# A fused attention and mixer kernel: weights decoded another way, a new plan for its first part, and a shifted slot table behind it

## The chip, the cores and the metric

The kernel runs on one core of a Trainium2 chip. The metric is the device time of one execution in microseconds (us), smaller being better. Six actors appear below by the profile's names: PE (TensorE, the matrix multiplies) with PEld (its weight loads, which run beside the multiplies), DVE (VectorE), ACT (ScalarE), POOL (GpSimd) and SP (SyncE, which issues DMA transfers here; its queue is SPq in the profile).

## The reference: what is computed

For 8 batches of 8 heads, 576 positions, 64 channels a head and 32 memory slots, attention goes through a small memory; then comes a token mixer and a channel mixer (here moe) with residuals:

```python
a = softmax(phi, axis=positions)                  # phi [8,8,576,32]
k_m = einsum('bhsm,bhsd->bhmd', a, k)             # and v_m from v
attn = softmax(scale * q @ k_m.T, axis=memory) @ v_m
x = attn.transpose(0, 2, 1, 3).reshape(8, 576, 512)
u = x + (relu(x.T @ w_tok1) @ w_tok2).T           # 576 -> 256 -> 576
out = u + relu(u @ w_ch1) @ w_ch2                 # 512 -> 1536 -> 512
```

q, k, v and phi are 32-bit floats; the four weight matrices arrive as 64-bit floats, so that each word takes 8 bytes of memory and has to be turned into a 32-bit float on the chip.

## The kernel before

**Arithmetic.** Each large product of two 32-bit operands is three products of shorter ones: a value is split in a high part (a rounding, made by ACT) and a low part (what is left, made by DVE or POOL), and high by high, high by low and low by high are added up in PSUM. In names, a final h is the high and a final l the low part (`uh`/`ul`, `hh`/`hl`, `c1h`/`c1l`).

**Weights.** A `Piece` brings one stretch of 64-bit words to SBUF (`rawc` for the channel mixer's w_ch1 and w_ch2, `raww` for the token mixer's), as two 32-bit words each, `low` and `high`. Six steps decode it in place: ACT takes the three top bits of the low word (`low_bits`, L638); DVE shifts the high word left by three and ors the three bits in (`join`, L643); ACT makes the sign from the high word by a steep Tanh (`signs`, L649); DVE clears the top bit and flips bit 30, which mends the exponent (`rebase`, L652); DVE clamps and multiplies by the sign (`apply`, L658); then ACT writes the high part (L665) and POOL the low part (L669) to the weight tiles. There are 4 pieces for w_tok1 and w_tok2 and 12 for the channel mixer, each of those one hidden block f of w_ch1 (512 words a partition in four transfers) together with the same block of w_ch2 (512 words in one transfer).

**Attention.** A `Quad` is four heads of one batch, 16 in all. Its steps on PE are kvp (memory keys and values from phi), Tp (a transpose), sp (scores; two PSUM tiles, one per half of the positions), Ap and Rp (token mixer's first product) and four u products (the token mixer's second product with the residual; each u is read out by ACT as `uh` or `rest` and by DVE as `ul`). Between sp and Ap stands the softmax: S turned and its maximum subtracted on DVE, exp on ACT, sum and multiplication on DVE; then the rows go out to DRAM and come back in another layout (`rows`, `raw`: L500, L505, L508), and ACT and DVE split them (`nat`, L118, L119). kvp, Tp, sp, Ap, Rp and u share two PSUM banks named `at` in turn.

**Channel mixer.** It runs over 9 chunks of 512 tokens and 12 hidden blocks: `cp` is the first product (L149, 12 matmuls into one of two `ch` banks), ACT and DVE read it out as `hh` (L122) and `hl` (L125), and `acc` is the second product (L188, 12 matmuls into four accumulating banks). At a chunk's end DVE adds the accumulators to the residual (`add`, L206), turns the layout and stores.

**Order.** All engines run their instructions in the program's order, which the kernel writes out by hand in two ways. The first part (batches 0 and 1, all weights, chunk 0) is a list of steps with costs, dependences and rooms (buffers); `plan(seed)` simulates the engines, gives each step a rank with some random noise from the seed, and emits the steps by their simulated begin. The rest goes by a table of half slots: a slot is one pair of products, `run(h, k)` calls what `at(h, fn, k=...)` put at half slot h, and the loop for a pair is

```python
high, low = chunks[c].ch1(f)          # cp
run(2 * g - 1, 1); high(); low()
run(2 * g, 0)                         # between cp and acc
before[0].ch2(before[1])              # acc of the block before
run(2 * g, 1); run(2 * g + 1, -1, 0)  # behind acc, ahead of the next cp
```

so an even half slot with k=0 lies between a cp and an acc, an odd one between an acc and the next cp. A quad of batches 2 to 7 has a first half slot r, and its steps stand at fixed distances from it. Quad (2,0) is planned half in the first part and has its r by itself.

## Time and profile before

| what | value |
|---|---|
| times of three runs | 820.14, 817.47, 820.19 us |
| median | 820.14 us |
| profiled execution | 819.32 us, of which 817.5 are the span from its first to its last instruction |
| busy in the span | PE 785.3, PEld 652.0, DVE 421.4, ACT 223.2, POOL 137.2 us |
| mean granted TensorE clock | 0.99 |

PE is busy for 96% of the span, so whatever shortens the run is either less work on PE or less time in which PE stands still or runs at a lower clock. A row of the timeline has the start, the duration, the engine, line and operation, the tiles written and read, the count, and in brackets how long the engine had been idle and what released it.

### The profile page before, as it was taken

How to read it: one execution, taken by the hardware profiler on the slowest of the kernel's cores; microseconds unless marked ns; L12 is line 12 of the kernel's file. 1: busy time of each engine (PE TensorE's matmuls, PEld its weight loads, DVE VectorE, ACT ScalarE, POOL GpSimd, SP SyncE). 2: the span in 40 equal slices, each digit the busy share in tenths (PEclk: the TensorE clock that was granted, in tenths of full speed). 3: DMA queues.
4: the chain of work that ended last, by engine and by line, in shares of the span. 5: the costliest groups of instructions: out<-in, count | busy, mean ns of one | idle time of the engine just before them, and what ended most of it. 6: DMA issues, size and time to landing. Idle time of an engine off the chain costs nothing.

```text
span 817.5 us, 12023 instructions
## 1 busy us (share of the span) xinstructions
PE 785.3 (96%) x4733; PEld 652.0 (80%) x4733; DVE 421.4 (52%) x699; ACT 223.2 (27%) x430; POOL 137.2 (17%) x136
## 2 busy tenths in 40 slices
PE   6698898999999999999999999999999999999997
PEld 4487677877887878787888888888878788888886
DVE  5898977385446543754456444744375313212115
ACT  4565645322222222222213221222123211210110
POOL 2135442300130002100121012101310300202000
PEclk9979999999999999999999999999999999999999
DMA  8999463035331522343323432252314100200202
GB/s 209 234 220 228 117 169 89 1 87 112 77 93 33 117 65 45 75 92 87 61 59 67 116 56 76 51 133 43 88 34 77 29 1 2 52 0 1 52 0 53
DMA packets 171128, 65.41 MB, mean 80 GB/s; under 512 B 112320, under 2 KB 168384, under 8 KB 171072
## 3 DMA queue, kind: packets, MB, share of 16 engines
q1 hardware_dynamic: 169984, 64.13, 35.1%
q8 instruction: 37, 0.61, 0.3%
q10 hardware_dynamic: 1088, 0.52, 0.3%
q14 instruction: 19, 0.16, 0.1%
HBM read 51.64 MB, written 12.98 MB: 79 GB/s over the span
## 4 chain that ended last, share of the span: by engine, by line
PE 87%; DVE 5%; SPq 3%; DMA 3%; issue 1%; ACT 1%; DVEq 0%; ACTq 0%
PE acc L188 34%; PE cp L149 34%; PE u L581 8%; PE Ap L541 3%; DMA rawc<-in_moe_w_ch_dram 2%; PE kvp L355 2%; PE sp L433 1%; PE Rp L560 1%; DVE rawc L643 1%; PE end L188 1%; SPq L926 1%; DVE rawc L658 1%; SPq L274 1%; DMA raww<-in_moe_w_tok_dram 1%; PE kvp L958 1%
## 5 line engine op out<-in xcount | busy, mean ns | idle before, releaser
L188 PE MATMUL acc<-hh,c 128*128 128x512 f32 x832 | 276.8, 394 | 0.0
L188 PEld LDWEIGHTS acc<-hh,c 128*128 128x128 f32 x832 | 157.2, 189 | 32.8 <-DVE o L206 0.5
L125 DVE SCALAR_TENSOR_TENSOR hl<-cp,hh 128x512 fp32r<-128x512 f32 x104 | 71.6, 689 | 203.7 <-ACT hh L122 203.6
L149 PE MATMUL cp<-uh,c1h 128*128 128x512 f32 x432 | 171.5, 397 | 0.0
L149 PE MATMUL cp<-ul,c1h 128*128 128x512 f32 x432 | 168.5, 390 | 0.0
L149 PE MATMUL cp<-uh,c1l 128*128 128x512 f32 x432 | 168.4, 390 | 0.0
L188 PE MATMUL acc<-hl,c 128*128 128x512 f32 x416 | 163.3, 393 | 2.2 <-DVE hl L125 2.2
L122 ACT ACTIVATE hh<-cp 128x512 fp32r<-128x512 f32 x104 | 62.2, 598 | 226.1 <-PE cp L149 226.1
L149 PEld LDWEIGHTS cp<-uh,c1h 128*128 128x128 f32 x432 | 81.1, 188 | 23.8 <-issue 8.2
L149 PEld LDWEIGHTS cp<-uh,c1l 128*128 128x128 f32 x432 | 81.1, 188 | 17.4
L149 PEld LDWEIGHTS cp<-ul,c1h 128*128 128x128 f32 x432 | 81.2, 188 | 15.5
L188 PEld LDWEIGHTS acc<-hl,c 128*128 128x128 f32 x416 | 78.6, 189 | 17.2 <-DVE hl L125 2.5
L200 POOL TENSOR_TENSOR o<-uh,ul 128x512 f32<-128x512 f32 x36 | 46.3, 1315 | 119.8 <-issue 70.7
L479 POOL TENSOR_TENSOR al<-aT,ah 128x576 fp32r<-128x576 f32 x16 | 23.3, 1455 | 255.9 <-issue 176.7
L594 ACT COPY rest<-u 128x288 f32<-128x288 f32 (+8 forms) x48 | 15.3, 320 | 93.0 <-PE u L581 92.0
L581 PE MATMUL u<-w2h,Rh 128*128 128x288 f32 x128 | 38.1, 298 | 0.0
L581 PE MATMUL u<-w2l,Rh 128*128 128x288 f32 x128 | 38.0, 297 | 0.0
L581 PE MATMUL u<-w2h,Rl 128*128 128x288 f32 x128 | 37.9, 296 | 0.0
L308 DVE TENSOR_REDUCE pr<-phi 128x128 f32<-128x640 f32 x27 | 35.1, 1302 | 5.2 <-DMA phi<-in_phi_dram 5.2
L602 DVE TENSOR_TENSOR ul<-u,uh 128x288 fp32r<-128x288 f32 (+8 forms) x48 | 16.8, 355 | 38.7 <-ACT uh L596 38.6
L541 PE MATMUL Ap<-w1h,nat 128*128 128x256 f32 x144 | 29.2, 294 | 1.5 <-DVE nat L1028 1.5
L441 DVE STREAM_TRANSPOSE S<-sp 128x288 f32<-128x288 f32 x32 | 15.0, 478 | 29.9 <-PE sp L433 28.9
(146 smaller groups left out, 968.8 us busy)
## 6 DMA issues: line engine op xcount, KB each, us to landing
out_dram<-rows SPq DMA_DIRECT2D x32, 256.0 KB, 4.8
kv<-in_k_dram SPq DMA_DIRECT2D x15, 512.0 KB, 4.2
kv<-in_v_dram SPq DMA_DIRECT2D x15, 512.0 KB, 5.5
q<-in_q_dram SPq DMA_DIRECT2D x192, 36.0 KB, 2.1
rawc<-in_moe_w_ch_dram SPq DMA_DIRECT2D x48, 128.0 KB, 5.6
rawc<-in_moe_w_ch_dram SPq DMA_DIRECT2D x12, 512.0 KB, 6.7
phi<-in_phi_dram SPq DMA_DIRECT2D x16, 256.0 KB, 4.5
rows<-S SPq DMA_DIRECT2D x48, 72.0 KB, 2.1
```

What stands on the lines that cost most here:

```text
L122: nc.scalar.activation(out=h, in_=ps, func=AF.Relu)
L125: nc.vector.scalar_tensor_tensor(out=l, in0=ps, scalar=0.0, in1=f32(h), op0=ALU.max, op1=ALU.subtract)
L149: nc.tensor.matmul(ps, l[:, a, w], r[:, a], start=a == 0 and x == 0, stop=a == NKK - 1 and x == 2,)
L188: nc.tensor.matmul(ps, l_[f // 2][:, f % 2, a * P : (a + 1) * P], r[:, w], start=f == start and x == 0, stop=f == end - 1 and x == 2,)
L200: nc.gpsimd.tensor_tensor(out=s.o[:, a], in0=f32(s.uh[:, a]), in1=f32(s.ul[:, a]), op=ALU.add)
L308: nc.vector.tensor_reduce(out=m.rearrange("p (i m) -> p i m", i=4), in_=s.pt.rearrange("p i j m -> p i m j"), axis=AX.X, op=op,)
L355: nc.tensor.matmul(s.kvp[32 * i : 32 * i + 32, : 2 * D], s.pt[:n, i, j, :], s.kv[i][:n, :, j, :], start=j == 0, stop=j == NC - 1,)
L479: nc.gpsimd.tensor_tensor(out=s.al, in0=s.aT, in1=f32(s.ah), op=ALU.subtract)
L541: nc.tensor.matmul(ps[:, :TT], a, w, start=x == 0, stop=x == len(mm) - 1)
L581: nc.tensor.matmul(ps[:, :HALF], a, r, start=x == 0, stop=x == len(mm) - 1)
L594: nc.scalar.copy(out=rest[0][:, kk, o : o + HALF - n], in_=ps[:, n:HALF])
L602: nc.vector.tensor_tensor(out=ch.ul[:, kk, to], in0=ps[:, :n], in1=f32(ch.uh[:, kk, to]), op=ALU.subtract)
```

## The change

It has five parts.

1. **Decoding.** ACT writes the three low bits as a float, 2.0 plus so many units of its last place, so that its word has bit 30 set and the three bits at the bottom; the join is an exclusive or, which then flips bit 30 by the way. What is left of `rebase` is clearing the top bit, a `magnitude`, which either DVE does (an AND) or ACT (Abs). The plan gives 7 of the 16 pieces to ACT: w_tok1's large piece, one of w_tok2's two pieces and five of the channel mixer.
2. **Pieces.** A piece of the channel mixer now holds two blocks of w_ch1 (1024 words, four transfers of twice the size) or two blocks of w_ch2. There are still 12.
3. **Planner.** It knows which steps of DVE and which of POOL it treats as excluding each other (`port`), some POOL steps may go to DVE, and the costs, the noise and the seed are others. Two low parts went to DVE, those of one w_ch1 piece and of one w_ch2 block; the low parts of the attention weights (`al`) all stay on POOL.
4. **Chunk 0's first product** runs its 12 matmuls sorted by product: the four that read `c1l` are last.
5. **Slot table.** The quads of batches 2 to 7, but for quad (2,0), have kvp, Tp and sp half a slot later, while nat, Ap, Rp and u stay at their half slots; sm2 (sum, division and the way through DRAM) goes from k=1 of an even half slot to k=0 of the odd one behind it, which is called right after it; only what stands there at k=-1 (the four additions `add`, at a chunk's end) comes in between. Quad (2,0) keeps kvp, Tp and sp and has what follows one half slot earlier.

```diff
-    mask = wp.tile([P, 6], F32, name="mask")
-    nc.gpsimd.memset(mask, 0.0)
+    mask = wp.tile([P, 7], F32, name="mask")
+    nc.gpsimd.memset(mask[:, :6], 0.0)
+    nc.gpsimd.memset(mask[:, 6:], 2.0)
...
+    two = mask[:, 6:]
...
         def mm_1(s, ps, f):
-            for a in range(NKK):
-                for x, (l, r) in enumerate(((c1h, s.uh), (c1h, s.ul), (c1l, s.uh))):
-                    nc.tensor.matmul(ps, l[:, a, w], r[:, a], ...)
+            mm = [
+                (a, x, l, r)
+                for a in range(NKK)
+                for x, (l, r) in enumerate(((c1h, s.uh), (c1h, s.ul), (c1l, s.uh)))
+            ]
+            if not s.c:
+                mm.sort(key=lambda m: m[1])
+            for n, (a, x, l, r) in enumerate(mm):
+                nc.tensor.matmul(ps, l[:, a, w], r[:, a], start=n == 0, stop=n == len(mm) - 1)
...
-        def a_low(s):
+        def a_low(s, eng=nc.gpsimd):
...
         def low_bits(s):
             nc.scalar.activation(
-                out=s.low, in_=s.low.bitcast(U32), func=AF.Copy, scale=THREE_BITS
+                out=f32(s.low), in_=s.low.bitcast(U32), func=AF.Identity,
+                scale=THREE_BITS * 2.0**-22, bias=two,
             )
 
         def join(s):
             nc.vector.scalar_tensor_tensor(
                 out=s.low, in0=s.high, scalar=3, in1=s.low,
-                op0=ALU.logical_shift_left, op1=ALU.bitwise_or,
+                op0=ALU.logical_shift_left, op1=ALU.bitwise_xor,
             )
...
-        def rebase(s):
-            nc.vector.tensor_scalar(
-                out=s.low, in0=s.low, scalar1=0x7FFFFFFF, scalar2=0x40000000,
-                op0=ALU.bitwise_and, op1=ALU.bitwise_xor,
-            )
+        def magnitude(s, eng):
+            if eng == "ACT":
+                nc.scalar.activation(out=f32(s.low), in_=f32(s.low), func=AF.Abs)
+            else:
+                nc.vector.tensor_scalar(
+                    out=s.low, in0=s.low, scalar1=0x7FFFFFFF, scalar2=None, op0=ALU.bitwise_and
+                )
...
     class PartC1:
-        words, loads, move = DM, 4, 2.8
+        words, loads, move = 2 * DM, 4, 4.4
 
         def __init__(s, f):
-            s.w, s.name = slice(f * P, (f + 1) * P), f"c_{f}"
+            s.w, s.name = slice(f * P, (f + 2) * P), f"c1_{f}"
...
         vary = random.Random(seed)
+        for z in steps:
+            z.eng, z.us = z.ways[0]
+            if z.ways[1] and vary.random() < SHARES[z.ways[1][0]]:
+                z.eng, z.us = z.ways[1]
+            z.port = z.shared and z.eng != "ACT"
...
-            t = free.get(z.eng, 0.0)
+            t = max(free.get(z.eng, 0.0), port if z.port else 0.0)
...
+            port = z.end if z.port else port
...
-    NOISE, SEED = 0.2, 192
+    NOISE, SEED = 0.3, 423
+    SHARES = {"DVE": 0.1, "ACT": 0.5}
...
-        z = step("DVE", vs, p.join, z, use=[raw])
+        z = step("DVE", vs, p.join, z, use=[raw], port=True)
         y = step("ACT", us, p.signs, z, use=[raw])
-        z = step("DVE", 0.15 + 0.6e-3 * p.words, p.rebase, z, use=[raw])
-        z = step("DVE", vs, p.apply, y, z, use=[raw])
+        z = step(
+            "DVE", 0.15 + 0.54e-3 * p.words, None, z, use=[raw], port=True, other=("ACT", us)
+        )
+        z.fn = lambda z=z: p.magnitude(z.eng)
+        z = step("DVE", vs, p.apply, y, z, use=[raw], port=True)
...
             l = step(
-                "POOL", 0.15 + 2.3e-3 * part.words, lambda x=x: p.part_low(x), h, use=[raw]
-            )
+                "POOL", 0.15 + 2.25e-3 * part.words, None, h, use=[raw], port=True,
+                other=("DVE", 0.08 + 1.15e-3 * part.words),
+            )
+            l.fn = lambda x=x, l=l: p.part_low(x, nc.vector if l.eng == "DVE" else nc.gpsimd)
...
-                homes[f], PartC1(f), PartC2(f), after=w_c[f - 5][1][:1] if f > 4 else (),
+                homes[f], *((PartC2(f - 1), PartC2(f)) if f % 2 else (PartC1(f),)),
+                after=w_c[f - 5][0][:1] if f > 4 else (),
...
-            r = 2 * NF * b - (15 if Q else 27)
+            r = 2 * NF * b - (14 if Q else 26)
             if b == 2 and not Q:
                 r = 2 * NF
...
             at(r, qd.step_kv)
             at(r + 1, qd.step_T)
             at(r + 2, qd.step_s)
-            at(r + 3, qd.sm2, k=1)
-            at(r + 7, qd.nat, k=1)
-            at(r + 9, qd.step_A)
-            at(r + 10, qd.step_R)
+            at(r + 3, qd.sm2)
+            at(r + 6, qd.nat, k=1)
+            at(r + 8, qd.step_A)
+            at(r + 9, qd.step_R)
             for x in range(4):
-                at(r + 11 + x, qd.step_u, x // 2, x % 2)
+                at(r + 10 + x, qd.step_u, x // 2, x % 2)
```

Two places in the table's part follow, and one in the planned part. In the rows, the numbers behind the names are the tile's own.

On PE, behind the last u of a quad (`u_3_1`, half slot 24b-1), before the change:

```order
L581 MATMUL u_3_1_3232<-w2h,Rh_1_3075 128x288
L581 MATMUL u_3_1_3232<-w2l,Rh_1_3075 128x288
L581 MATMUL u_3_1_3232<-w2h,Rl_1_3076 128x288
L433 MATMUL sp_4_0_3245<-qT_0_3188,kb_0_3209 32x288 x4
L433 MATMUL sp_4_0_3246<-qT_0_3188,kb_0_3209 32x288 x4
L149 MATMUL cp_3_3262<-uh_2713,c1h 128x512
L149 MATMUL cp_3_3262<-ul_2714,c1h 128x512
```

and the same quad's scores after it:

```order
L157 MATMUL cp_3_3207<-uh_2680,c1h 128x512
L157 MATMUL cp_3_3207<-ul_2681,c1h 128x512
L157 MATMUL cp_3_3207<-uh_2680,c1l 128x512
L435 MATMUL sp_4_0_3229<-qT_0_3183,kb_0_3201 32x288 x4
L435 MATMUL sp_4_0_3230<-qT_0_3183,kb_0_3201 32x288 x4
L190 MATMUL acc_2_2522<-hh_2_3118,c_1535 128x512
L190 MATMUL acc_2_2522<-hl_2_3119,c_1535 128x512
```

The scores stood right behind a u product and ahead of a cp; now a transpose (not shown) and a whole cp stand between, and an acc follows.

On DVE, from the turn of these scores on, before:

```order
L441 STREAM_TRANSPOSE S_0_3255<-sp_4_0_3245 128x288
L441 STREAM_TRANSPOSE S_0_3255<-sp_4_0_3246 128x288
L448 TENSOR_REDUCE mx_0_3258<-S_0_3255 128x18
L451 TENSOR_TENSOR S_0_3255<-S_0_3255,mx_0_3258 128x576
L125 SCALAR_TENSOR_TENSOR hl_3_3276<-cp_3_3262,hh_3_3275 128x512
L460 TENSOR_REDUCE sm_0_3291<-S_0_3255 128x18
L461 TENSOR_SCALAR sm_0_3291<-sm_0_3291 128x18
L462 RECIPROCAL sm_0_3291<-sm_0_3291 128x18
L465 TENSOR_TENSOR S_0_3255<-S_0_3255,sm_0_3291 128x576
L471 STREAM_TRANSPOSE aT_0_3304<-S_0_3255 128x576
L206 TENSOR_TENSOR o_3120<-acc_2_2555,o_3120 128x512
L206 TENSOR_TENSOR o_3120<-acc_2_2556,o_3120 128x512
```

and after:

```order
L443 STREAM_TRANSPOSE S_0_3239<-sp_4_0_3229 128x288
L443 STREAM_TRANSPOSE S_0_3239<-sp_4_0_3230 128x288
L450 TENSOR_REDUCE mx_0_3242<-S_0_3239 128x18
L453 TENSOR_TENSOR S_0_3239<-S_0_3239,mx_0_3242 128x576
L208 TENSOR_TENSOR o_3087<-acc_2_2522,o_3087 128x512
L208 TENSOR_TENSOR o_3087<-acc_2_2523,o_3087 128x512
L208 TENSOR_TENSOR o_3087<-acc_2_2524,o_3087 128x512
L208 TENSOR_TENSOR o_3087<-acc_2_2525,o_3087 128x512
L462 TENSOR_REDUCE sm_0_3262<-S_0_3239 128x18
L463 TENSOR_SCALAR sm_0_3262<-sm_0_3262 128x18
L464 RECIPROCAL sm_0_3262<-sm_0_3262 128x18
L467 TENSOR_TENSOR S_0_3239<-S_0_3239,sm_0_3262 128x576
```

The four additions to the accumulators (`o`) came behind the softmax's sum and turn, and now come ahead of them. `hl` (L125) of the next block stood in between and now comes behind.

On DVE in the planned part, around the first `hl`, before:

```order
L652 TENSOR_SCALAR rawc_371<-rawc_371 128x1024
L943 TENSOR_REDUCE mc_0_715<-mt_0_689 128x1
L945 TENSOR_SCALAR dg_0_717<-ident,mc_0_715 128x128
L658 SCALAR_TENSOR_TENSOR rawc_371<-rawc_371 128x1024
L643 SCALAR_TENSOR_TENSOR rawc_420<-rawc_420 128x1024
L643 SCALAR_TENSOR_TENSOR rawc_454<-rawc_454 128x1024
L125 SCALAR_TENSOR_TENSOR hl_0_739<-cp_0_701,hh_0_738 128x512
```

and after:

```order
L604 TENSOR_TENSOR ul_591<-u_0_1_669,uh_590 128x224
L659 TENSOR_SCALAR rawc_0_372<-rawc_0_372 128x1024
L664 SCALAR_TENSOR_TENSOR rawc_0_372<-rawc_0_372 128x1024
L961 TENSOR_REDUCE mc_0_723<-mt_0_682 128x1
L963 TENSOR_SCALAR dg_0_725<-ident,mc_0_723 128x128
L127 SCALAR_TENSOR_TENSOR hl_0_721<-cp_0_690,hh_0_720 128x512
```

Two joins and an apply that stood right ahead of the first `hl` are gone from there; one AND and one apply stand further up.

More of the change, by code (lines that the diff above doesn't have):

```diff
@@ L368, in scales @@
             nc.vector.reciprocal(out=sm, in_=sm)
[L369 removed]
+            nc.vector.tensor_scalar_mul(out=s.ms, in0=mask[:, :6], scalar1=sm)
             s.per = sm
@@ L751 @@
     class PartC2:
-        words, loads, move = DM, 1, 2.4
+        words, loads, move = DM, 1, 2.2
         held = []
@@ L792, with __init__ @@
     class Step:
-        def __init__(s, eng, us, fn, after, take, use, move):
+        def __init__(s, eng, us, fn, after, take, use, move, port, other):
             s.eng, s.us, s.fn, s.after, s.take, s.move = eng, us, fn, list(after), take, move
+            s.port = s.shared = port or eng == "POOL"
+            s.ways = [(eng, us), other]
             s.begin = s.end = s.ready = None
@@ L803, with step @@
     steps = []
-    def step(eng, us, fn, *after, take=(), use=(), move=0.0):
-        steps.append(Step(eng, us, fn, after, list(take), list(use), move))
+    def step(eng, us, fn, *after, take=(), use=(), move=0.0, port=False, other=None):
+        steps.append(Step(eng, us, fn, after, list(take), list(use), move, port, other))
         return steps[-1]
```

39 lines of the change are left out of this document (17 added, 22 removed).

## The prediction

> **What bounds the kernel now.** I read the page first, then the busy time by stretches, then what PE waits for in each, then the timeline at these waits.
>
> ```profile
> PE 785.3 (96%) x4733; PEld 652.0 (80%) x4733; DVE 421.4 (52%) x699; ACT 223.2 (27%) x430; POOL 137.2 (17%) x136
> 0.00:59.70 59.70, 42.46 (x381) 36.38 (x382) 45.71 (x74) 32.16 (x60) 14.04 (x30) 0.91 0.97 223
> 59.70:159.70 100.00, 91.96 (x606) 75.45 (x607) 74.47 (x99) 52.96 (x87) 42.38 (x31) 0.98 0.51 126
> 159.70:802.00 642.30, 641.40 (x3676) 531.02 (x3675) 292.42 (x509) 138.06 (x284) 80.75 (x76) 1.00 0.28 60
> 39.80:49.90 10.10, 8.55 (x38) 8.09 (x38) 9.20 (x11) 5.44 (x9) 4.61 (x4) 0.50 1.11 230
> 98.00:101.00 3.00, 3.00 (x9) 2.32 (x9) 2.96 (x6) 2.39 (x5) 1.29 (x2) 0.50 0.00 0
> ```
>
> Ahead of the stretches' engines (PE, PEld, DVE, ACT, POOL) stands the length, behind them the granted clock, the DMA share and GB/s. Three stages with different limits: up to 59.7 us DMA is at 0.97 of its time and PE idles 17 us, so the first product waits for loads and decoding. From there to 159.7 PE idles 100 - 91.96 = 8.0 us and has a stretch at half clock. Behind it PE idles 0.9 us in 642, and only its own rows can hide a loss. PE's matmul count does not change in any of them, so the sum is made of waits.
>
> ```profile
> PE mt L939 <- DVE nat L1028: 2.5, 1, 2.5
> PE acc L188 <- DVE hl L125: 2.2, 1, 2.2
> PE u L581 <- DVE Rl L125: 1.7, 1, 1.7
> PE np L1015 <- DVE phi L322: 0.9, 1, 0.9
> PE mt L939 <- DVE pr L308: 0.5, 1, 0.5
> PE u L581 <- DVE mc L943: 0.5, 1, 0.5
> PE u L581 <- DVE ul L602: 0.3, 1, 0.3
> PEld sp L433 <- DVE ul L602: 3.0, 4, 0.9
> PEld sp L433 <- ACT rest L594: 2.8, 7, 0.4
> ```
>
> The first seven are PE's waits from 59.7 to 159.7, all on DVE, 8.6 in all against 8.0 of idle time, since a wait can begin beside a matmul's end; the last two are weight loads' waits behind 159.7, which the busy share hides because a matmul row runs on while its loads wait.
>
> **The slot table.** Scores as they run unhindered (169.96), and behind a u whose readout by ACT they await (420.98); the row at 189.79 closes six products:
>
> ```profile
> 169.96 0.71 PE L433 MATMUL sp<-qT,kb 64*32 64x288 f32 x16
> 170.60 0.50 PE L188 MATMUL acc<-hh,c 128*128 128x512 f32 x1
> 173.47 0.39 PE L149 MATMUL cp<-uh,c1h 128*128 128x512 f32 x1
> 189.79 0.28 PE L541 MATMUL Ap<-w1h,nat 128*128 128x256 f32 x1
> 420.98 1.25 PE L433 MATMUL sp<-qT,kb 64*32 64x288 f32 x16
> 421.08 0.40 ACT L594 COPY rest<-u 128x288 f32<-128x288 f32 x1 [3.47 <-PE u L581]
> 421.53 0.15 PEld L433 LDWEIGHTS sp<-qT,kb 64*32 64x32 f32 x8 [0.40 <-ACT rest L594]
> 422.15 0.50 PE L149 MATMUL cp<-uh,c1h 128*128 128x512 f32 x1
> ```
>
> The second score tile needs the bank of the u just issued. From their start to the next product's, the scores take 0.64 us at 169.96 and 1.17 at 420.98. By the two rows on sp, 4 + 7 = 11 of the twelve quads from (2,0) on wait, 5.8 us together. The change puts a whole cp between u and scores in ten of them, and its 2.7 us outlast the readout (0.40 us on ACT; DVE's share is of that size, since no wait is over 0.9). In quad (2,1) a u still stands ahead, and up to 0.9 remains. Gain 5.8 - 0.9 = 4.9; I take 5. It may be 6.2, since each loses some 0.13 more than its wait (1.17 - 0.64 - 0.40), ten times. It may be 3.5, if the transpose Tp, now right behind the last u, waits 0.15 in each for its operand from DVE: T is written one product ahead of it now as before, so I take this for the bound only.
>
> What is late next is nat, for which Ap waits; here the moved steps lose room:
>
> ```profile
> 167.71 2.45 DVE L206 TENSOR_TENSOR o<-acc,o 128x512 f32<-128x512 f32 x4
> 174.93 0.75 DVE L460 TENSOR_REDUCE sm<-S 128x18 f32<-128x576 f32 x1
> 177.12 1.99 SPq L500 DMA_DIRECT2D rows<-S  x4
> 184.39 1.05 DVE L119 TENSOR_TENSOR nat<-raw,nat 128x512 fp32r<-128x512 f32 x2
> ```
>
> From the sum's start to nat's end it is 184.39 + 1.05 - 174.93 = 10.5 us, with the rows' way through DRAM in it: four writes issued at 177.12, two reads behind their landing. In the first quads of batches 3 to 7 the four additions (2.45 us on DVE) now precede the sum. They need the acc behind the scores to end, and that took 173.47 - 170.60 = 2.87. So nat is ready 2.87 + 2.45 + 10.5 = 15.8 us behind the scores. Between scores and Ap stand this acc and five products; six products took 189.79 - 173.47 = 16.3, so one is 2.72, and the room is 2.87 + 5 x 2.72 = 16.5. The slack is 0.7 us (before, the sum did not wait for an acc and the room was a product longer). Nothing is moved past another transfer: SP's issues behind the first part stand in the same order, with these writes ahead of the next quad's q. The second quads have no additions and some 2 us of slack. Expected loss 0; where landing takes a microsecond longer, Ap waits for the rest, in five quads.
>
> **The first part.** First the wait of `acc` at the first block:
>
> ```profile
> 65.40 0.48 PE L188 MATMUL acc<-hh,c 128*128 128x512 f32 x1
> 65.05 2.33 DVE L643 SCALAR_TENSOR_TENSOR rawc<-rawc 128x1024 int32<-128x1024 int32 x1
> 67.30 0.68 DVE L125 SCALAR_TENSOR_TENSOR hl<-cp,hh 128x512 fp32r<-128x512 f32 x1
> 68.03 0.50 PE L188 MATMUL acc<-hl,c 128*128 128x512 f32 x1 [2.16 <-DVE hl L125]
> 70.66 0.39 PE L149 MATMUL cp<-uh,c1h 128*128 128x512 f32 x1
> ```
>
> This acc took 70.66 - 65.40 = 5.27 us from start to start, 2.4 to 2.55 more than one that waits for nothing (2.87 or 2.72). `hl` stood behind an apply and two joins; in the changed order the joins are elsewhere, and the maximum `mc` and the small product `dg` come between the apply and it: 2.2 us saved. Of the other six waits the two large ones had their cause in the order of PE: the transpose of phi (mt) behind a pair of np tiles, whose banks it had to get back from nat (2.5), and the u products right behind a cp that follows Rp (1.7). In the changed order an acc stands between the np tiles and the next attention step, and an acc between each Rp and the next u. The four small ones (2.2 together) have a product in between in most cases. What comes instead I followed through the changed order of DVE, ACT and POOL with these durations:
>
> ```profile
> L643 DVE SCALAR_TENSOR_TENSOR rawc<-rawc 128x1024 int32<-128x1024 int32 x12 | 18.0, 1503 | 5.0 <-ACT rawc L638 5.0
> L658 DVE SCALAR_TENSOR_TENSOR rawc<-rawc 128x1024 f32<-128x1024 f32 x12 | 18.1, 1506 | 1.2 <-ACT rawc L649 0.8
> L652 DVE TENSOR_SCALAR rawc<-rawc 128x1024 int32<-128x1024 int32 x12 | 10.4, 863 | 0.2
> L638 ACT ACTIVATE rawc<-rawc 128x1024 int32<-128x1024 uint32 x12 | 13.7, 1146 | 2.6 <-issue 1.4 <-DMA rawc<-in_moe_w_ch_dram 1.3
> L649 ACT ACTIVATE rawc<-rawc 128x1024 int32<-128x1024 f32 x12 | 13.9, 1161 | 3.2 <-DVE rawc L643 3.2
> L669 POOL TENSOR_TENSOR c1l<-rawc,c1h 128x512 fp32r<-128x512 f32 x12 | 17.8, 1484 | 51.9 <-ACT c1h L665 33.5 <-DMA rawc<-in_moe_w_ch_dram 16.5 <-DMA q<-in_q_dram 1.9
> ```
>
> I find 0.2 on a low part of w_ch2, 0.1 on phi's exp, 0.5 on Tp, and allow 2 more for joins that a POOL step stretches (2.33 us at 65.05 against a mean of 1.50). Waits of 8.0 become 2.8, and the half clock goes with the wait of 2.5 us right ahead of it: at 98.00 PE is busy for 3.0 us at 0.50, which costs 1.5. That is 5.2 + 1.5 = 6.7, taken as 6.5; the bounds are 9.5 (no wait, full clock) and 0 (as many new waits as old ones).
>
> The prices of the edits themselves: DVE loses seven `rebase` (five at 0.86, one large and one small at about 0.8), 6 us, and gains two low parts, 2 to 3 us. ACT gains seven Abs like the Tanh beside them, five at 1.16 and two at up to that, some 7.6 us, and saves a start on six joined CASTs. Over 0 to 159.7 ACT is busy 32.16 + 52.96 = 85.1 us; with 93 it still idles 40%, and this idle time is the cover. If it is gone, see the ACT rival. The Identity in place of the Copy is priced as Tanh, 1161 against 1146 ns: nothing. Here the Trainium skill, "ScalarE: Activation LUTs", in the section on what a table load costs, speaks against the change: an operand given by a pointer, as the bias `two` is, adds about 93 ns to an activation; by it ACT would have 1.5 us more in 16 pieces, an estimate from that page, which no run here shows and which the same idle time would cover. Sorting chunk 0's first product moves no work: 0. Fewer, larger transfers move the same bytes under a DMA share of 0.97: 0.
>
> Before the first product, PE waits longest at the first of these rows, right ahead of the half clock, and last at the second:
>
> ```profile
> 38.99 0.44 PE L1015 MATMUL np<-ident,aT 128*128 128x128 f32 x2 [3.22 <-DVE aT L471]
> 59.61 0.33 PE L939 MATMUL mt<-ident,pr 128*128 128x128 f32 x1 [0.49 <-DVE pr L308]
> ```
>
> In the changed order the last u's readout, not this maximum (`pr`), stands last ahead of the first product on DVE, so the 0.49 goes, and the second quad's nat comes earlier on DVE while its aT comes later. I take 1 us off. The bounds are 1 us more (aT later by one step of DVE, nothing won) and 3.3 us less (two thirds of the 10.1 us at half clock from 39.80 on run at full clock, which halves them).
>
> **Sum:** 5 + 6.5 + 1 = 12.5 us off the profiled 819.3 gives 806.8; the median of the runs shown is 0.8 above it. I say 807.
>
> **The rivals.**
>
> - *The first part gives its gain back.* A plan's durations leave out what the trace shows, such as a join of 2.33 us where POOL works. Then only the table's 5 us stay: 814.3. For it: all seven waits were on DVE, and the plan can be off by a microsecond at any of 23 products. Against: DVE has 3 to 4 us less to do in a stretch where it idles a quarter. 0.12.
> - *Ap waits in place of the scores.* With rows home a microsecond or more late in five quads: 806.8 + 5 to 6 = 812.5. For it: a slack of 0.7. Against: no Ap waits behind 159.7 in the trace of before. 0.10.
> - *Full clock throughout.* If the wait of 3.2 us for aT, which ends where the half clock sets in, becomes shorter, PE keeps its clock from 39.80 on. It was busy 8.55 us there at half speed, so up to 4.3 us are won, of which loads (DMA at 1.11) take back a part: some 3 us, 803.7. For it: aT's place on DVE has changed. Against: aT still comes behind the joins of the first weights. 0.12. The Trainium skill, "TensorE: Matmul & The Clock Gate", Part 1 on the clock gate, states a free-running window of 3413 ns, with half speed behind a window without work and full speed behind a busy one; by that rule, this case happens once the wait no longer fills a window. The trace agrees as far as it goes: 10.1 us at half speed are about three such windows, behind a wait of 3.2.
> - *The change does nothing.* Every wait is replaced, and an engine that is busy 96% stays so: 820. Against: the scores' waits depend on the order alone. 0.05.
> - *Slower: ACT's queue becomes the wait.* `hh` stands in ACT's order among Abs, CASTs and Tanh of over a microsecond each; a late `hh` delays `hl` and the acc behind it by as much as at 65.40, 2.55 us. The change is off the gain from five late ones on (12.5 / 2.55), slower than can be told from seven on, and with nine of twelve it is 819.3 - 12.5 + 23 = 830. For it: ACT gets 7.6 us more of work. Against: it idles 47 of the 100 us. 0.04.
>
> My forecast has 0.57. The first, second and fourth case lie at 812 and above and the third a little below it, so the range goes from 802 (4.8 of the 6.6 that the favourable bounds, 1.3 + 3.0 + 2.3, give together) to 815.5, which leaves out the fourth and fifth and the far ends. A measurement of this kernel can tell 0.5%, 4.1 us, from no change: faster is below 816. The first three cases and the forecast make 0.91, less 0.04 for the first one's upper edge: faster 0.87; same 0.08; slower 0.05.
>
> **What would show it.** In the changed profile: scores that take 0.65 us start to start in all quads but (2,1), and no wait of their loads on `rest`; PE idle of 2 to 4 us in the hundred behind the first product; DVE's magnitude in nine pieces; PE never waiting for nat behind 160. It is wrong if PE waits for `hh` in several blocks of chunk 0, if Ap waits for nat, or if the first product begins over 2 us later than at 59.71.

## The result, and the profile after

The changed kernel takes 804.47 us in the median of four runs (804.24 to 804.88), the kernel before 819.96 in the runs beside it: a ratio of 0.9823, with a 95% interval of 0.9808 to 0.9839. The prediction was 807.0, in a range of 802.0 to 815.5. The profiled execution took 804.88 us, of which 803.1 are the span: 14.4 less than the one before. Some executions were disturbed and took at least a fifth longer; all times here are medians of the others, and where the profiled execution was a disturbed one (the slot table alone, and the changed kernel once more) the stages are missing.

First the page's busy times and its stretches, cut where the stages change: ahead of the first product of chunk 0 (57.2 us), from there to the scores of quad (2,0) (161.9), and behind them. The stretch at 39.5 is where the half clock was.

```profile
PE 777.0 (97%) x4737; PEld 646.4 (80%) x4737; DVE 410.2 (51%) x694; ACT 230.7 (29%) x431; POOL 136.1 (17%) x129
0.00:57.20 57.20, 41.51 (x385) 34.22 (x386) 41.61 (x70) 36.68 (x63) 14.99 (x31) 0.97 0.97 236
57.25:161.94 104.69, 100.72 (x723) 82.43 (x723) 75.50 (x112) 57.49 (x90) 35.46 (x23) 1.00 0.51 129
161.90:787.60 625.70, 625.34 (x3558) 520.56 (x3558) 284.29 (x496) 136.47 (x279) 85.60 (x76) 1.00 0.28 60
39.50:50.00 10.50, 7.47 (x58) 7.03 (x57) 9.48 (x11) 8.60 (x14) 4.82 (x4) 1.00 1.04 272
```

The order is PE, PEld, DVE, ACT, POOL, then the granted clock, the DMA share and GB/s. PE's idle time in the middle stage is 104.69 - 100.72 = 4.0 us, and the clock is 1.00 there and at 39.5, where it had been 0.50. ACT has 7.5 us more to do over the run, DVE 11 less. The prediction counted 7.6 and 3 to 4: it took DVE's rows at their old durations, and joins, applies and some other steps are shorter in the mean here.

Next what PE waits for in the middle stage (us in total, times, longest):

```profile
PE sp L1021 <- ACT qT L1011: 1.3, 1, 1.3
PE Ap L543 <- DVE nat L1046: 1.2, 1, 1.2
PE mt L957 <- DVE pr L310: 0.9, 1, 0.9
PE Tp L986 <- DVE vb L392: 0.6, 1, 0.6
PE qt L1003 <- issue: 0.4, 1, 0.4
PE qp L998 <- ACT kb L990: 0.4, 1, 0.4
```

And from the timeline three of the twelve pairs of scores, the last two with the product behind them:

```profile
161.94 0.72 PE L435 MATMUL sp<-qT,kb 64*32 64x288 f32 x16
197.75 0.69 PE L435 MATMUL sp<-qT,kb 64*32 64x288 f32 x8
198.81 0.69 PE L435 MATMUL sp<-qT,kb 64*32 64x288 f32 x8 [0.36 <-DVE ul L604]
199.43 0.50 PE L190 MATMUL acc<-hh,c 128*128 128x512 f32 x1
412.56 0.71 PE L435 MATMUL sp<-qT,kb 64*32 64x288 f32 x16
413.21 0.50 PE L190 MATMUL acc<-hh,c 128*128 128x512 f32 x1
```

None of the seven waits of before is in this list, but for mt on pr. That one stands just ahead of the first product, at 57.16 us, so the stage itself has the other five, some 4 us in all. The scores take 413.21 - 412.56 = 0.65 us to the next product in eleven quads of twelve. Only quad (2,1), at 197.75, still has a u right ahead and takes 1.68.

The span falls into three stages by two events that every profile here has: the first product of chunk 0, and quad (2,0)'s scores, which are the first step of the slot table that is the same in all kernels. Starts are those of the timeline's rows; the last column is the span less the scores' start.

| kernel | first product at | middle stage | scores of (2,0) at | rest |
|---|---|---|---|---|
| before | 59.71 | 110.25 | 169.96 | 647.5 |
| changed | 57.25 | 104.69 | 161.94 | 641.2 |
| difference | -2.5 | -5.6 | -8.0 | -6.4 |

### The profile page after: what moved, and what is told of

It reads as the page before. It is cut to its first block, busy times and chain, and to the rows that moved or that the text cites. A ratio compares the mean times of both kernels' runs of the same rounds, so it can differ in the third digit from the quotient of the medians.

```text
span 803.1 us, 11970 instructions
## 1 busy us (share of the span) xinstructions
PE 777.0 (97%) x4737; PEld 646.4 (80%) x4737; DVE 410.2 (51%) x694; ACT 230.7 (29%) x431; POOL 136.1 (17%) x129
## 4 chain that ended last, share of the span: by engine, by line
PE 88%; DMA 4%; DVE 3%; SPq 3%; issue 1%; ACT 1%; DVEq 0%; ACTq 0%
PE cp L157 35%; PE acc L190 35%; PE u L583 8%; PE Ap L543 3%; DMA rawc<-in_moe_w_ch_dram 2%; PE kvp L357 2%; DMA phi<-in_phi_dram 1%; PE Rp L562 1%; PE end L190 1%; SPq L944 1%; PE sp L435 1%; DVE rawc L647 1%; SPq L276 1%; SPq L280 0%; DVE rawc L664 0%
## 5 line engine op out<-in xcount | busy, mean ns | idle before, releaser
L190 PEld LDWEIGHTS acc<-hh,c 128*128 128x128 f32 x832 | 156.2, 188 | 39.4 <-issue 7.3
L157 PE MATMUL cp<-uh,c1h 128*128 128x512 f32 x432 | 164.7, 395 | 0.0
L157 PE MATMUL cp<-ul,c1h 128*128 128x512 f32 x432 | 162.8, 390 | 0.0
L157 PE MATMUL cp<-uh,c1l 128*128 128x512 f32 x432 | 162.3, 389 | 0.0
L157 PEld LDWEIGHTS cp<-uh,c1h 128*128 128x128 f32 x432 | 80.4, 188 | 16.4 <-issue 0.9
L202 POOL TENSOR_TENSOR o<-uh,ul 128x512 f32<-128x512 f32 x36 | 46.1, 1308 | 117.3 <-DMA out_dram<-rows 46.7
L343 POOL PARTITION_ALL_REDUCE psr<-pr x11 | 17.4, 1585 | 78.1 <-PE cp L157 68.2
```

The lines of the kernel that those rows point to most:

```text
L157: nc.tensor.matmul(ps, l[:, a, w], r[:, a], start=n == 0, stop=n == len(mm) - 1)
L190: nc.tensor.matmul(ps, l_[f // 2][:, f % 2, a * P : (a + 1) * P], r[:, w], start=f == start and x == 0, stop=f == end - 1 and x == 2,)
L202: nc.gpsimd.tensor_tensor(out=s.o[:, a], in0=f32(s.uh[:, a]), in1=f32(s.ul[:, a]), op=ALU.add)
L343: nc.gpsimd.partition_all_reduce(s.r, m, P, RED.add)
```

## The experiments

Twelve runs, in three groups, each group on one chip with runs of the kernel before between them. Ratios are to these, with a 95% interval. All stages are in one table behind the last group.

### Parts apart

**The slot table alone**, on the kernel before:

```diff
-            r = 2 * NF * b - (15 if Q else 27)
+            r = 2 * NF * b - (14 if Q else 26)
...
-            at(r + 3, qd.sm2, k=1)
-            at(r + 7, qd.nat, k=1)
-            at(r + 9, qd.step_A)
+            at(r + 3, qd.sm2)
+            at(r + 6, qd.nat, k=1)
+            at(r + 8, qd.step_A)
```

> The kernel before with the new slot table alone; its first part is unchanged. Theory (the two parts add): from quad (2,0) on to the end the changed kernel was 6.4 us shorter than before (641.2 against 647.5 us), 6.2 of it in the scores, so here the same: 6.0 to 6.5 us less than before, a ratio of 0.992 to 0.993, with scores of 0.65 us start to start everywhere but in quad (2,1). Rival (the table's gain leans on the first part, since the first part's stores and loads of batch 2 run into it): under 4 us, and waits of Ap or kvp behind 160 us.

Measured: 812.32 us against 819.58, a ratio of 0.9913 (0.9883 to 0.9943). **The first part alone**, the changed kernel with these lines turned back:

> The changed kernel with the old slot table; its first part is the changed one. Theory (the parts add): the first product begins 2.5 us earlier (57.2) and quad (2,0)'s scores 8 us earlier than before (162 against 170), then the scores cost as much as before: 7.5 to 8.5 us less than before, a ratio of 0.990 to 0.991. Rival: over 10 us less, if the remaining clock loss of before (half clock around 40 and 98 us) is worth more than the profile's 8 us.

Measured: 811.90 us, 0.9913 (0.9881 to 0.9945). The two gains, 7.3 and 7.7 us, add up to 14.9 before rounding, and the changed kernel has 15.5: the parts add, as far as intervals of 5 us tell. The profiles tell more. The first part alone leaves a rest of 647.6 us, that of before to 0.1; every kernel with the new table and without a further edit has 641.1 to 641.2. So the table is worth 6.4 us, whatever stands ahead of it.

**The planner alone**, on the kernel before: decoding, pieces, first product and slot table are old, but DVE's port steps (the ones that the change marks) and POOL's exclude each other in the plan, and the seed is the best of some 3000 by its planned end. The planner also takes the changed kernel's noise and its costs for the decoding steps, which are 2 to 8% lower; the lines below leave the costs out.

```diff
-            t = free.get(z.eng, 0.0)
+            t = max(free.get(z.eng, 0.0), port if z.port else 0.0)
...
+            port = z.end if z.port else port
...
-        z = step("DVE", vs, p.join, z, use=[raw])
+        z = step("DVE", vs, p.join, z, use=[raw], port=True)
...
-    NOISE, SEED = 0.2, 192
+    NOISE, SEED = 0.3, 1661
```

> The kernel before with its own decoding, pieces and slot table, but planned by a planner that lets DVE's port steps and POOL's steps exclude each other (with the changed kernel's costs for them), under the seed with the best planned end of some 3000. Its plan puts the first product at 58.8 and the last second product of chunk 0 at 152.4 us. The kernel before was planned at 56.0 and 150.9 and ran at 59.7 and 155.7: 3.7 and 4.8 late. The changed kernel was planned at 58.4 and 149.5 and ran at 57.2 and 147.6: 1.2 and 1.9 early. Theory P (the planner's knowledge of the exclusion is the first part's gain): it runs where it is planned or a little earlier, the last second product begins at 150.5 to 152.5, so 3 to 5 us less than before. Rival D (the gain is the lighter decoding on DVE): it stays within 1.5 us of before, 155 or later.

Measured: 812.00 us, 0.9921 (0.9889 to 0.9952): 7.6 us less, more than theory P asked for, and all of what the whole first part brings. **The reverse**, the changed kernel planned without the exclusion:

```diff
-            z.port = z.shared and z.eng != "ACT"
+            z.port = False
...
-    NOISE, SEED = 0.3, 423
+    NOISE, SEED = 0.3, 2507
```

> The changed kernel with all of its decoding, pieces and slot table, but planned without the exclusion of DVE's port steps and POOL's, under the seed with the best planned end of some 2000. Its plan puts the first product at 57.0 and the last second product of chunk 0 at 148.1 us, ahead of the changed kernel's own plan (58.4 and 149.5). Theory P: it runs 4 to 5 us behind its plan as the kernel before did, the last second product begins at 152 to 153, so it is 4 to 6 us slower than the changed kernel, around 809. Rival D (the lighter decoding is the gain): it runs as the changed kernel, 804 to 805.

Measured: 806.52 us, 0.9848 (0.9805 to 0.9890), 2.1 above the changed kernel's median, with intervals that overlap; theory P had asked for 809. The rows of the scores of (2,0), of the first of these kernels and then of the second:

```profile
162.57 0.71 PE L433 MATMUL sp<-qT,kb 64*32 64x288 f32 x16
```

```profile
166.01 0.72 PE L435 MATMUL sp<-qT,kb 64*32 64x288 f32 x16
```

They begin 7.4 and 4.0 us before those of before (169.96). Theory P had the direction of both against their plans, not the sizes: the first begins its last second product at 148.4, 4.0 ahead of its plan (152.4) and ahead of the range expected; the second at 151.7, 3.6 behind (148.1), less than the 4 to 5 expected. Rival D falls as it was put, since the old decoding gets the whole gain.

That the exclusion by itself makes the gain is not shown. With the old decoding no run separates it from the costs and the noise. In the reverse run, which keeps those, the times don't tell a loss, and in the profile what it loses lies ahead of the first product (62.16, where five kernels with the same first part have 55.3 to 59.0); its middle stage of 103.85 us is no longer than the changed kernel's 104.69. Of the 7.4 us of the first kernel, too, 5.3 lie ahead of the first product (54.45 against 59.71) and 2.1 behind it. Nor are its joins shorter than those of before, which took 1503 ns in the mean:

```profile
L643 DVE SCALAR_TENSOR_TENSOR rawc<-rawc 128x1024 int32<-128x1024 int32 x12 | 19.2, 1603 | 4.0 <-ACT rawc L638 2.4 <-DMA rawc<-in_moe_w_ch_dram 1.6
```

### Seed, clock and the one pair of scores left

**The kernel before under another seed** of its own planner:

```diff
-    NOISE, SEED = 0.2, 192
+    NOISE, SEED = 0.2, 387
```

> The kernel before with nothing changed but the seed of its plan: the one of 3000 with the best planned end by its own planner (which knows nothing of the exclusion of DVE and POOL). Its plan puts the first product at 55.9 and the last second product of chunk 0 at 149.0 us, 1.9 ahead of the plan of before (150.9). The run planned without the exclusion but with the new decoding was 4.0 us ahead of before at quad (2,0)'s scores. Theory S (that was the seed: a search over more seeds finds a luckier plan): this one is 2 to 5 us less than before too, its last second product begins at 151 to 153.5 us. Theory D' (that was the lighter decoding): it runs within 1.5 us of before or slower, the last second product at 154 or later, 5 or more behind its plan.

Measured: 820.12 us against 818.68, a ratio of 1.0019 (1.0001 to 1.0037). Planned 1.9 us ahead of before, it begins its last second product at 156.5, 7.5 us behind its plan and 0.8 behind before. The best planned of 3000 seeds is worth nothing to the old planner; theory S falls as it was put, by this one seed.

**Planner and slot table together**, with old decoding, pieces and first product, and under the planner's second-best seed (1113):

> The kernel before with its own decoding and pieces, planned with the exclusion of DVE's port steps and POOL's, under the seed with the second best planned end (first product planned at 58.6, last second product at 152.7), and with the new slot table. Theory P (planner and slot table are the whole gain, decoding and pieces are worth nothing by themselves, and any well placed seed will do): 804 to 806.5 us, as the changed kernel, a ratio of 0.981 to 0.984; the last second product 2 to 4 us ahead of its plan, at 148.5 to 151. Rival (the seed run before was a lucky one, or the decoding is worth something): 808 or more, the last second product behind 152.

Measured: 804.64 us, 0.9838 (0.9807 to 0.9869), against the changed kernel's 804.47 and 0.9823. Its last second product begins at 147.6, 5.1 ahead of its plan, where 2 to 4 had been expected. Two of the five parts, the planner without its choice of engines and the slot table, bring the whole gain as far as the intervals tell, and under a second seed.

**The clock.** In the kernel before, 13 more idle matmuls fill the wait of 3.2 us ahead of the second quad's np:

```diff
                 z.fill = int(0.42 * gap / 0.24)
             idle = z.end
+    c.x_n.fill += 13
     for z in order:
         now[0] = z
```

> The kernel before with 13 more idle matmuls (identity by identity, into a bank that np takes next) ahead of the second quad's np, so that PE works through its wait of 3.2 us for aT at 36 to 39 us. Nothing else moves. Theory: the half clock from 39.7 to 49.9 us comes from the nearly idle stretch before it, so it goes, PE's own work there (8.6 us at half speed) takes some 4 us less, but the first product waits for decoded weights and for DVE as well: 1 to 2.5 us less than before, the first product at 57.2 to 58.7. Rival 1 (the clock is not the limit there at all): first product within 0.5 us of 59.7 at full clock, no gain. Rival 2 (the clock falls for another reason): half clock stays at 39.7.

Measured: 818.24 us against 818.68, 0.9992 (0.9969 to 1.0015): no gain that shows, in an interval from 2.5 us less to 1.2 more. Its stretches, in the columns as above:

```profile
32.70:36.10 3.40, 3.40 (x17) 2.54 (x14) 3.07 (x6) 1.25 (x3) 1.42 (x1) 0.50 1.09 224
36.10:39.50 3.40, 3.40 (x31) 3.40 (x30) 1.93 (x5) 2.62 (x4) 0.00 (x0) 0.94 1.08 235
39.50:43.00 3.50, 3.50 (x33) 3.50 (x32) 3.40 (x5) 2.19 (x5) 1.44 (x2) 1.00 1.09 230
43.00:46.40 3.40, 0.76 (x6) 0.56 (x6) 3.23 (x5) 1.48 (x3) 1.96 (x2) 1.00 1.16 207
46.40:50.00 3.60, 3.60 (x19) 3.60 (x19) 3.57 (x5) 2.21 (x3) 1.29 (x2) 0.55 1.10 218
50.00:53.00 3.00, 3.00 (x25) 3.00 (x24) 2.53 (x4) 2.37 (x5) 0.00 (x0) 0.98 1.11 226
```

And the wait for nat and the first product in its timeline:

```profile
45.86 0.51 PE L541 MATMUL Ap<-w1h,nat 128*128 128x256 f32 x2 [2.64 <-DVE nat L1028]
...
60.44 0.47 PE L149 MATMUL cp<-uh,c1h 128*128 128x512 f32 x1
```

Behind the filled stretch the clock is full at 39.5, so the fall at 39.7 did come from the nearly idle stretch, and rival 2 is out. PE then waits for nat longer, 2.64 us where it had been 1.55. That leaves 43.0 to 46.4 with 0.76 us of work, and the next 3.6 us run at 0.55. The first product begins at 60.44, no earlier than at 59.71.

That is not yet rival 1, because this execution was late before the filler. Its clock is at 0.50 in 32.7 to 36.1, where the kernel before has 1.00. On ACT, `Ah` waits for PE's slowed Ap, the exp of S stands behind it, and DVE waits for the exp:

```profile
36.85 0.37 ACT L1036 CAST Ah<-Ap 128x256 fp32r<-128x256 f32 x1 [2.90 <-PE Ap L541]
37.12 0.69 ACT L456 ACTIVATE S<-S 128x576 f32<-128x576 f32 x1
37.84 0.75 DVE L460 TENSOR_REDUCE sm<-S 128x18 f32<-128x576 f32 x1 [1.37 <-ACT S L456]
40.00 0.78 DVE L471 STREAM_TRANSPOSE aT<-S 128x576 f32<-128x576 f32 x1
45.13 0.99 DVE L1028 TENSOR_TENSOR nat<-np,nat 128x512 fp32r<-128x512 f32 x2
```

The last two of them in the kernel before:

```profile
38.15 0.78 DVE L471 STREAM_TRANSPOSE aT<-S 128x576 f32<-128x576 f32 x1
43.29 0.99 DVE L1028 TENSOR_TENSOR nat<-np,nat 128x512 fp32r<-128x512 f32 x2
```

From aT to nat it is 5.13 us in the filled kernel and 5.14 before, although PE's clock is full in one until 46.7 us and falls to half at 39.7 in the other. On this way DVE is the limit, and a faster PE waits for it. But aT begins 1.85 us later here, and from nat to the first product it is 15.3 us against 16.4. So rival 1 holds for the way to nat; what a full clock is worth for the whole stage, neither this profile nor the times tell.

The Trainium skill, "TensorE: Matmul & The Clock Gate", Part 1 on the clock gate, has half speed behind an idle free-running window of 3413 ns and full speed behind a busy one. The rises, at 50.0 us before and at 36.5 and 50.1 here, stand behind 3.4 us that are full of work. The falls, at 39.7 before and at 29.7 and 46.7 here, stand behind 3.4 us with 0.7, 1.1 and 0.8 us of work, so the trace agrees if an idle window need not be empty.

**Quad (2,0)'s last two u products half a slot later**, in the changed kernel, so that none stands ahead of quad (2,1)'s scores:

```diff
-                at(r + 10 + x, qd.step_u, x // 2, x % 2)
+                at(r + 10 + x + (r == 2 * NF and x > 1), qd.step_u, x // 2, x % 2)
```

> The changed kernel with quad (2,0)'s last two u products one half slot later, so that no u stands ahead of quad (2,1)'s scores, the one place where the scores still take 1.67 us from start to start instead of 0.65. Theory: 1.0 us less than the changed kernel, all scores at 0.65, about 803.4. Rival: the wait goes to the moved u's or to Ap of quad (2,1), no gain.

Measured: 802.93 us, 0.9820 (0.9782 to 0.9858). The pair that took 1.68 us:

```profile
195.68 0.71 PE L435 MATMUL sp<-qT,kb 64*32 64x288 f32 x16
196.32 0.50 PE L190 MATMUL acc<-hh,c 128*128 128x512 f32 x1
```

It takes 0.64 now, and the rest is 640.2 us instead of 641.2. The 1.0 us is shown by the stage; by the times alone it is not, as the group below says.

### On one chip with the changed kernel

**The changed kernel once more:**

> The changed kernel itself, beside the three others on one chip, to compare them with: 804 to 805 us, a ratio of 0.981 to 0.984; its first product begins between 56 and 59 us, as it did at 57.2 here, 59.0 and 55.9 in two kernels with the same first part.

Measured: 803.23 us against 817.53, 0.9821 (0.9790 to 0.9851).

**Its order held, but magnitudes all on DVE and chunk 0's first product unsorted:**

```diff
-        z.fn = lambda z=z: p.magnitude(z.eng)
+        z.fn = lambda: p.magnitude("DVE")
...
-            if not s.c:
-                mm.sort(key=lambda m: m[1])
```

> The changed kernel with its order of steps held, but all magnitudes as an AND on DVE (seven Abs less on ACT, some 7.6 us, seven ANDs more on DVE, some 6 us) and without the sorting of chunk 0's first product. Theory P (the order that the plan finds is the gain; which engine makes the magnitude and the sorting are worth little): within 2 us of the changed kernel, 804 to 806.5, the first product within the 56 to 59 us that equal first parts show. Rival D (DVE is the engine that holds the first part back, and ACT's share of the decoding is what lightens it): 5 to 6 us slower, 809 to 811, with new waits of PE on hl, nat or join.

Measured: 805.63 us, 0.9843 (0.9816 to 0.9871), 2.4 above the changed kernel, a little over the 2 of theory P, in intervals that overlap. Its middle stage, to be held against the changed kernel's row of 57.25 to 161.94 above:

```profile
58.33:163.07 104.74, 100.97 (x723) 82.37 (x723) 77.52 (x116) 54.13 (x88) 35.16 (x23) 1.00 0.51 128
```

ACT has 3.4 us less there, DVE 2.0 more, and the stage is as long to 0.05 us. The first product is at 58.33, inside of what equal first parts show (55.3 to 59.0 in the table). Who makes the magnitude, and whether the product is sorted, moves nothing that can be measured. Rival D's 809 to 811 did not come.

**A later softmax**, some 2.3 us in five quads:

```diff
-            nc.vector.tensor_reduce(out=s.sm, in_=s.S, axis=AX.X, op=ALU.add)
+            for _ in range(4 if s.b > 2 and not s.Q else 1):
+                nc.vector.tensor_reduce(out=s.sm, in_=s.S, axis=AX.X, op=ALU.add)
```

> The changed kernel with the softmax's sum made four times instead of once on DVE in the first quads of batches 3 to 7, which delays their nat by three times 0.75 us, 2.25. Theory (nat is ready only some 0.5 us ahead of Ap in these five quads, 0.80, 0.31, 0.68, 0.07 and 0.65 by the changed kernel's trace, 1.6 to 2.4 in the others): Ap waits 1.7 us for nat in each, 8.7 us in all, so 812 to 814. Rival (there is other room, a DMA landing that hides it or an S that is waited for anyway): under 3 us.

Measured: 811.86 us, 0.9928 (0.9904 to 0.9952), 8.6 above the changed kernel; the rest is 649.2, 8.0 more, 1.6 in each of the five quads. The size is about as expected (8.7), the place is not. From the timeline of one quad, starts in us:

```profile
247.19 3.10 DVE L463 TENSOR_REDUCE sm<-S 128x18 f32<-128x576 f32 x4
251.63 0.78 DVE L474 STREAM_TRANSPOSE aT<-S 128x576 f32<-128x576 f32 x1
252.44 0.67 ACT L478 CAST ah<-aT 128x576 fp32r<-128x576 f32 x1 [6.84 <-DVE aT L474]
253.02 1.08 ACT L124 ACTIVATE hh<-cp 128x512 fp32r<-128x512 f32 x2
253.66 0.51 PE L190 MATMUL acc<-hh,c 128*128 128x512 f32 x1 [0.78 <-ACT hh L124]
```

And what the weight loads wait for behind 161 us, in all five quads:

```profile
PEld acc L190 <- ACT hh L124: 6.0, 5, 1.2
PEld acc L190 <- DVE hl L127: 2.7, 5, 0.5
PEld Ap L544 <- DVE nat L121: 0.2, 1, 0.2
```

`ah`, the split of the softmax's turned tile, stands ahead of `hh` in ACT's order. It waits for aT, `hh` waits behind it, and the acc waits for `hh` and `hl` long before Ap would wait for nat. Once acc has paid 1.6 us, nat is in time to 0.2 us.

**The u products apart, once more:**

> The changed kernel with quad (2,0)'s last two u products one half slot later, once more, beside the changed kernel on the same chip. It had 802.9 us, 1.5 less than the changed kernel's four times. Theory: 1.0 us less than the changed kernel, that is the one pair of scores that took 1.67 us instead of 0.65. Rival: no difference from it, the 1.5 having been the first part's spread.

Measured: 803.00 us, 0.9811 (0.9772 to 0.9851), 0.2 below the changed kernel on this chip, with intervals that overlap. Its rest is 640.2 again. The 1.0 us is shown by the stage in two profiles; the times cannot tell it from the spread.

### All stages

| kernel | first product at | middle stage | scores of (2,0) at | rest | last second product, planned | measured |
|---|---|---|---|---|---|---|
| before | 59.71 | 110.25 | 169.96 | 647.5 | 150.9 | 155.7 |
| before, other seed | 59.12 | 111.65 | 170.78 | 648.0 | 149.0 | 156.5 |
| before, wait filled | 60.44 | 109.99 | 170.44 | 647.5 | 150.9 | 156.2 |
| planner alone | 54.45 | 108.11 | 162.57 | 647.6 | 152.4 | 148.4 |
| planner and slot table | 58.06 | 103.77 | 161.83 | 641.2 | 152.7 | 147.6 |
| changed, planned without exclusion | 62.16 | 103.85 | 166.01 | 641.1 | 148.1 | 151.7 |
| changed | 57.25 | 104.69 | 161.94 | 641.2 | 149.5 | 147.7 |
| first part alone | 59.03 | 104.92 | 163.95 | 647.6 | 149.5 | 149.6 |
| changed, plain decoding | 58.33 | 104.74 | 163.07 | 641.2 | 149.5 | 148.8 |
| changed, u apart, twice | 55.92, 55.34 | 105.11, 105.23 | 161.03, 160.57 | 640.2, 640.2 | 149.5 | 146.7, 146.3 |
| changed, late sum | 55.77 | 104.71 | 160.48 | 649.2 | 149.5 | 146.2 |

Plans that know the exclusion are kept or beaten, by up to 5.1 us and never missed by more than 0.2. The three plans that don't are missed by 3.6 to 7.5. Kernels with the same first part differ by 3.4 us in the last column (146.2 to 149.6), so the sides are clear and the single differences are not.

## Why the prediction was right, step by step

The sum was 5 + 6.5 + 1 = 12.5 us; the profiles have 6.4, 5.6 and 2.5, 14.4 before rounding. All three signs were right and the total is 1.9 short, but the terms are off by 1.4, -0.9 and 1.5, and the third came by another way than I gave.

**The slot table** was right in mechanism and mis-sized by 1.4: I took the waits (5.8 - 0.9) and put what the scores lose from start to start, some 0.13 more in each, into the bound of 6.2 only, which the measured 6.4 just passes. The scores of the twelve quads took 15.0 us before and take 8.8 now, 6.2 less. The start-to-start time is the price: a weight load's wait of 0.40 us cost 0.53 (1.17 - 0.64) at 420.98. Where the other 0.13 goes, no run shows.

**Nat's slack** was forecast at 0.7 us for the first quads of batches 3 to 7. In the changed kernel nat ends 0.80, 0.31, 0.68, 0.07 and 0.65 us ahead of Ap's start. Ap waits in none, and the rival on Ap did not happen. What I named as late next was the wrong step: with some 2.3 us more on the way, `hh` behind `ah` on ACT pays first.

**The first part's waits** were said to go from 8.0 to 2.8, and are 4.0. The `hl`, nat and `Rl` waits went as argued, and Tp's 0.6 was forecast at 0.5. Two I had not found: scores that wait for qT from ACT (1.3), and an Ap for nat (1.2). The half clock's 1.5 us went with the wait of 2.5, as said, so the stage has 4.1 + 1.5 = 5.6. The seven waits add up to 8.6 against 8.0 of idle time because the 0.5 of mt on pr ends at 59.61, ahead of the stage, and not for the reason that I gave. What I left out is how the new order was found. I told it by the waits that the order avoids and laid stretched joins to a rival's account ("A plan's durations leave out what the trace shows"). The changed planner does reckon with them, by letting these steps exclude each other. The rows of before for one join beside POOL and one alone:

```profile
94.32 1.59 POOL L479 TENSOR_TENSOR al<-aT,ah 128x576 fp32r<-128x576 f32 x1 [5.38 <-ACT ah L475]
94.57 2.43 DVE L643 SCALAR_TENSOR_TENSOR rawc<-rawc 128x1024 int32<-128x1024 int32 x1
114.09 1.23 DVE L643 SCALAR_TENSOR_TENSOR rawc<-rawc 128x1024 int32<-128x1024 int32 x1 [2.52 <-ACT rawc L638]
```

POOL's step ends at 95.91; the join, at 97.00, 1.1 later, about what it takes alone. The Trainium skill, "SBUF — State Buffer", section "SBUF: two separate sides", states a port pair that DVE, with two operands in SBUF, and GpSimd hold in turn for a whole instruction; the trace agrees. What the planner as a whole is worth here the planner-alone run shows, 7.6 us by the times; how much of that is the exclusion stays open, as said there.

**The prices of the edits**: two that I put at nothing are nothing in the stage, since with the order held, magnitudes on DVE and no sorting leave it at 104.7 us. The larger pieces were not run by themselves. One row that I set aside was right, though it changes no sum: I priced the Identity as a Tanh. In the group rows of the changed kernel, it and the Abs are

```profile
L641 ACT ACTIVATE rawc<-rawc,mask 128x1024 f32<-128x1024 uint32 x12 | 14.9, 1242 | 2.5 <-DMA rawc<-in_moe_w_ch_dram 2.5
L657 ACT ACTIVATE rawc<-rawc 128x1024 f32<-128x1024 f32 x5 | 5.7, 1146 | 0.0
```

1242 ns against the Copy's 1146, 96 more. The Trainium skill, "ScalarE: Activation LUTs", section "What ACT_TABLE_LOAD costs", has about 93 for an operand given by a pointer. The estimate of 1.5 us in 16 pieces that I worked out from it holds, and it doesn't show in the time: the kernel with planner, slot table and the old Copy is not faster than the changed one (804.64 against 804.47).

**Before the first product** I said 1 us; this pair of profiles has 2.5. Five kernels with the same first part have it between 55.3 and 59.0, so a single pair doesn't measure this term. Its reason failed: the wait for `pr` did not go. It was 0.49 us and is 0.88 at 57.16, and between 0.47 and 1.81 in the five kernels. What did become shorter is the wait for aT, from 3.22 us to 2.14 (2.14 to 2.17 in the five kernels), and with it came the condition of the full-clock rival: the clock is 1.00 at 39.5. That rival had 803.7 us, the forecast 807, and the measured 804.47 lies nearer to the rival; the forecast's range covered both. How much of the 2.5 us the clock made is open, since the filled wait could not price it.

**Left open:** which part of the planner makes the first part's gain, the exclusion, the costs or the noise; and why the new decoding planned without the exclusion still gained 4.0 us at the scores. The lighter work on DVE is one possible cause of that, and the costs, the noise and the seed are others; no run here separates them. Also open is what moves the first product by 3.7 us between kernels with the same first part.

## What to carry to other kernels

Before searching for a better order, hold the planner's times against the trace: the old planner's two plans ran 4.8 and 7.5 us behind, and a better planned end under another seed gained nothing; with two engines' exclusion and new costs in the planner, the same old steps took 7.6 us less. A step that needs the bank of the instruction just ahead of it is cheapest moved behind a long one, and its price is read from start to start of the products around it, not from the wait's bracket. When room is taken from a chain, look at every instruction that queues behind its steps, on ACT too: the first to be late need not be the chain's own end.

## What the runs showed of the hardware that was not expected

Equal instructions in equal order reach the first product between 55.3 and 59.0 us, while the 640 us behind quad (2,0)'s scores repeat to 0.1 us between kernels with the same slot table (before under its other seed is the one exception, 648.0 against 647.5). And what a half clock costs depends on the engine that holds the chain: on the way from aT to nat, where DVE is busy throughout, it cost nothing (5.13 us with the clock full, 5.14 with a fall to half on the way), while a half clock from 32.7 to 36.1 us in the filled kernel held PE's Ap, ACT's exp behind it and so DVE, which waited 1.37 us.
